# One pass of cluster products for the two-token pairs of the first batch, and a new order for the first quarter of the program

## The chip, the cores and the metric

The kernel runs on one core of one Trainium2 chip. A core has five engines, each with a queue of its own that it works through in order: TensorE (PE: matrix products, whose weight loads are shown apart as PEld), VectorE (DVE), ScalarE (ACT), GpSimd (POOL) and SyncE (SP, which issues most transfers). They wait for each other through semaphores. The metric is the device time of the one launch in microseconds (us), the median of the runs taken; lower is better.

## The reference

Two layers follow each other. The first is attention restricted by clusters, for 4 batches, 8 heads, 768 tokens and head size 64: every query and every key goes to the nearest of 16 centroids of its head (by cosine), and a query only sees keys of its own cluster.

```python
q_assign = np.argmax(np.einsum('bhsd,hcd->bhsc', q_n, c_n), axis=-1)
k_assign = np.argmax(np.einsum('bhsd,hcd->bhsc', k_n, c_n), axis=-1)
mask = q_assign[:, :, :, None] == k_assign[:, :, None, :]
scores = np.where(mask, scale * np.matmul(q, k.transpose(0, 1, 3, 2)), -1000000000.0)
attn = softmax(scores)            # written out with max, exp and sum
x = np.matmul(attn, v)            # then heads side by side: 3072 tokens x 512
```

The second layer takes each of the 3072 tokens through `h = x @ w_in` (512 to 1024), `u = h * softmax(h)`, a normalisation of u over its 1024 columns with gain `g_ln`, and `@ w_out` (1024 to 512).

## The kernel before, in words

**Tiles.** Work on q and k goes by pair: two heads of one batch, so 4 batches x 4 pairs. For each pair the kernel needs q and k with the head dimension on the partitions, as bf16, in a tile `qk` of its own (six of them in turn). Under the 64 rows of the head stand up to 32 further rows: the one-hot code of the token's cluster. A product over these 80 or 96 rows is then the score plus a constant (256) where query and key share a cluster, and the exponential's bias takes the constant away again; keys of other clusters vanish. That is the mask.

**From loaded q and k to scores.** The first batch (4 pairs) differs from the other three. Its pair 0 is prepared in two halves, from 64x64 transposes on PE (line 396). Pairs 1, 2 and 3 of the first batch are the ones that the change speaks of: each partition holds 12 tokens' data in one long row, which PE turns in 128x128 blocks (line 403, "tp" in the order), two tokens to a block, so the turned tile `xt` holds even tokens in its upper 64 rows and odd tokens in its lower 64, and the two heads lie side by side in its columns. The code calls them `twelve`; "two-token pairs" is meant by that. In the other batches DVE turns the data by itself (line 444), and the two heads lie one above the other.

For a pair the steps are, with the name each has in the order: copy out of PSUM into `xt` (xa, xb; lines 422 and 430; ACT or DVE), cast into `qk` (ca; lines 468 to 472; ACT, DVE or POOL), products with the centroids into the PSUM tile `csc` (cl; PE), a turn of `csc` in 32x32 blocks (tb; line 497; DVE), the maximum over each group of 16 (mx; line 510; DVE), the one-hot code (oh; line 515; DVE), a turn back (ot; line 521; DVE), four copies of the code into `qk` (pl; lines 533 to 540; POOL, DVE or a transfer), and a memset that blanks the 16 rows that belong to the other head (bl; line 549). Scores are S (line 627, PE), their exponential E (line 635, ACT), the product with v is V (line 654, PE), the division by the sum N (lines 666 and 679, DVE). In the second layer, h and y are PE's products, hm, u, bn and ag are DVE's, ex is ACT's, at and al are POOL's, sc is the scaling of the output.

In the products with the centroids (lines 475 to 492) four products stand beside each other in four 32-column strips of PE's array. For a two-token pair that takes two rounds, one for each head (`hh`), that add up in PSUM: 8 products of 384 columns. Lines 912 to 916 make the weights for it, 128 columns for each pair.

**Order.** Nothing is scheduled at run time. Every step is an entry with an engine, needs and a planned cost; the strings `ORDER` (line 28 on) say for each engine in which order kinds of steps stand in its queue, and `AWAY` moves single steps to another engine. `ca0.0.0.1.0` reads: cast, batch 0, pair 0, q, head 1, half 0. The costs and keys in the `add` calls only tell the recording layer in which sequence to write the program; an engine's own queue is set by `ORDER` and `AWAY` alone.

**Start.** Until the first q and k have landed, PE runs products of zeros (`idle`, line 859) into a PSUM tile that nobody reads: the step wm (25 of them, each 128 columns, with a weight load of 128 columns before each) and single steps fl of two each.

Of the kernel before, what the change touches and what calls it, by code (L numbers as in the profile page):

```python
# [22 lines left out]
class Weave:  # L23
# [6 lines left out]
        ld4 si ld3 lv lg ld3 lo lv lo ld2 lo2 lv ld6 lv ld8 li4 tx ld3 lv ld tx lv tu ld10 tx tu ld4  # L30
        tu lv ld ou lv ld3 tu ld3 ou ld8 ou2 ld2 tu ld5 tx lv2 ld pl tu ld10 tx ld5 ou2 tu lv tx lv
        tu ld9 ou tu ld4 lv2 ld4 pl tu ou tx ld3 tu tx ld4 ou tu2 ou lv tx lv ou pl3 tu3 ou tx2 ou2
        tu tx tu tx tu ou2 tx ou tu2 ou tu ou6
    """
    ORDER["POOL"] = """
        pl2 bl pl3 ca pl ca cv ca3 pl3 bl ca pl ca pl cv z2 pl3 ca bl z cv2 ca pl4 sg bl cv2 wi ca
        wi7 ca3 at pl4 z cv ca2 cv bl cv al pl2 ca3 at pl2 z bl ca3 al at al pl4 at ca cv ca cv ca
        cv al bl ca3 pl4 ca2 pl4 at2 pl2 bl ca cv pl al2 ca2 cv2 ca2 at cv ca4 al pl4 at2 cv bl cv3
        pl2 al pl2 ca2 bl ca at al ca pl2 cv2 pl ca3 al ca3 pl at2 pl3 al2 ca2 pl ca at cv pl cv at
        ca at cv al pl2 bl pl al at3 al2 at al2 at al at al2 at2 po at al3  # L40
    """
    ORDER["PE"] = """
# [126 lines left out]
def kernel(  # L169
# [80 lines left out]
    def used(hh):  # L250

        return slice(0, D + NC_) if hh == 0 else slice(0, D + 2 * NC_)
# [603 lines left out]
    def idle(n):  # L856

        for _ in range(n):
            nc.tensor.matmul(idle_p[:, :P], idle_w, idle_w)  # L859
# [465 lines left out]
```

## Time and profile before

| | |
|---|---|
| time, three runs | 223.49, 223.98, 224.14 us; median 223.98 |
| profiled execution: span from first to last instruction | 222.4 us |
| PE, DVE, ACT, POOL busy | 97%, 90%, 88%, 57% of the span |
| TensorE clock granted over the span | 0.999 |
| chain that ended last | PE 91%, DVE 3%, ACT 2%, issue 2% |

The profiled execution carries no time of its own beside its span; the median of the runs is 1.6 us above that span, which is what lies before the first and behind the last instruction together with the difference between executions. A row of a timeline gives start, length, engine, line, operation, output and inputs with sizes, and how many such instructions were merged; "x16" for 8 products is right, since each product of fp32 data leaves two records. Busy time counts an instruction from its start to its end, and ends of neighbours overlap, so the busy shares lie a little above the share of time in which an engine could have taken nothing more.

### The profile page before, as it was taken

The page shows a single profiled execution, that of the slowest core. Times are in us where ns is not written, and L with a number is a line of the kernel's source. Part 1 is how long each engine was busy: PE and PEld are TensorE (multiplying, and loading weights), DVE is VectorE, ACT ScalarE, POOL GpSimd, SP SyncE. Part 2 cuts the span into 40 slices and gives each one's busy share as a digit, 9 for nine tenths or more (in the row PEclk, how much of TensorE's full clock was granted, in tenths as well). Part 3 has the DMA queues.
Part 4 walks back from the last instruction along what each step waited for, and adds up shares of the span by engine and source line. Part 5 has one row for each costly group of instructions (what it writes and reads, how often), then busy time and mean ns, then how long its engine had stood idle before and what let it go on. Part 6 is the DMA issues. An engine that isn't in the chain of part 4 may idle for free.

```text
span 222.4 us, 6852 instructions
## 1 busy us (share of the span) xinstructions
PE 214.8 (97%) x2518; PEld 151.8 (68%) x2548; DVE 199.1 (90%) x363; ACT 194.7 (88%) x382; POOL 126.6 (57%) x252
## 2 busy tenths in 40 slices
PE   8999899999999999999999999999999999999993
PEld 7765577767777687777777666676767767665452
DVE  2789999999999999899989999999999979999891
ACT  3899999999999999999999989999999989795352
POOL 3189597759884986188837674783746101226131
PEclk9999999999999999999999999999999999999999
DMA  6998989797799979899999897998922928565623
GB/s 157 352 388 221 193 165 284 203 172 165 127 175 237 180 141 215 136 193 166 153 211 239 156 185 150 151 168 158 230 99 50 115 78 145 117 165 121 166 98 143
DMA packets 122433, 38.74 MB, mean 174 GB/s; under 512 B 111448, under 2 KB 117152, under 8 KB 122400
## 3 DMA queue, kind: packets, MB, share of 16 engines
q1 hardware_dynamic: 121680, 37.82, 79.8%
q10 hardware_dynamic: 720, 0.49, 0.7%
q8 instruction: 20, 0.33, 0.7%
q14 instruction: 13, 0.11, 0.1%
HBM read 23.11 MB, written 6.29 MB: 132 GB/s over the span
## 4 chain that ended last, share of the span: by engine, by line
PE 91%; DVE 3%; issue 2%; ACT 2%; DVEq 0%; ACTq 0%
PE sps L627 27%; PE hreg L744 18%; PE yps L813 17%; PE ops L654 16%; PE csc L489 4%; PE hreg L627 2%; PE idle_p L859 2%; PE csc L484 1%; PE hreg L403 1%; PE hreg L396 1%; ACT qk L468 1%; PE hreg L813 1%; ACT e L635 1%; DVE u L763 1%; DVE w_sum L598 1%
## 5 line engine op out<-in xcount | busy, mean ns | idle before, releaser
L635 ACT ACTIVATE e<-sps 128x512 bf16<-128x512 f32 (+1 forms) x276 | 143.2, 609 | 10.2 <-PE sps L627 9.8
L627 PE MATMUL sps<-qk 96*128 96x256 bf16 (+5 forms) x600 | 87.4, 263 | 0.7 <-ACT e L635 0.4
L627 PEld LDWEIGHTS <-qk 96*128 96x128 bf16 (+1 forms) x636 | 59.6, 121 | 24.5 <-issue 8.8
L654 PEld LDWEIGHTS <-e 128*128 128x128 bf16 x1152 | 49.9, 97 | 9.3 <-issue 1.9
L654 PE MATMUL ops<-v,e 128*128 128x65 bf16 x1152 | 54.3, 193 | 0.4 <-DVE x L679 0.4
L744 PE MATMUL hreg<-w_in_sb,xT 128*128 128x512 bf16 x177 | 48.3, 378 | 0.8
L813 PE MATMUL yps<-w_out_c,uT 128*128 128x512 bf16 x169 | 45.1, 379 | 0.8
L540 POOL COPY qk<-oht 32x384 f32<-32x384 f32 (+1 forms) x49 | 24.2, 494 | 21.5 <-DVE oht L521 15.7
L763 DVE TENSOR_TENSOR u<-e_sb,hreg 128x1024 bf16<-128x1024 bf16 (+1 forms) x25 | 29.1, 1169 | 2.7 <-ACT e_sb L756 2.1
L774 DVE BATCH_NORM_STATS2 bs<-u 128x6 f32<-128x512 bf16 x48 | 31.3, 677 | 0.0
L750 DVE TENSOR_REDUCE nmax<-hreg 128x1 f32<-128x1024 f32 x24 | 29.1, 1213 | 2.0 <-PE hreg L744 1.7
L756 ACT ACTIVATE e_sb<-hreg,nmax 128x1024 bf16<-128x1024 f32 x24 | 26.9, 1121 | 4.5 <-DVE nmax L750 4.4
L790 POOL TENSOR_SCALAR esq<-es,mv 128x1 f32<-128x1 f32 x24 | 8.3, 344 | 33.6 <-DVE mv L778 30.3
L813 PEld LDWEIGHTS <-uT 128*128 128x128 bf16 x200 | 18.0, 97 | 13.1 <-issue 0.3
L744 PEld LDWEIGHTS <-xT 128*128 128x128 bf16 x192 | 17.6, 97 | 11.3 <-ACT e L635 0.3
L472 POOL TENSOR_SCALAR qk<-xt 64x768 bf16<-64x768 f32 (+1 forms) x27 | 22.2, 823 | 3.5 <-DVE xt L444 1.7
L444 DVE STREAM_TRANSPOSE xt<-raw 128x768 f32<-128x768 f32 x24 | 22.2, 949 | 0.0
L470 POOL CAST qk<-xt 64x768 bf16<-64x768 f32 (+1 forms) x25 | 20.9, 836 | 1.2
L679 DVE TENSOR_TENSOR x<-ops,den 128x256 bf16<-128x256 f32 (+1 forms) x39 | 18.9, 486 | 1.3
L784 POOL TENSOR_SCALAR es<-esum 128x1 f32<-128x1 f32 x24 | 5.6, 236 | 20.9 <-ACT e_sb L756 20.4
L793 POOL TENSOR_TENSOR alpha<-esq,halves 128x1 f32<-128x1 f32 x24 | 13.8, 574 | 2.0
L830 ACT ACTIVATE y<-yps,alpha 128x512 f32<-128x512 f32 x15 | 10.4, 695 | 4.3 <-PE yps L813 3.0
(85 smaller groups left out, 206.9 us busy)
## 6 DMA issues: line engine op xcount, KB each, us to landing
vf<-in_v_dram SPq DMA_DIRECT2D x16, 384.0 KB, 4.6
out_dram<-y SPq DMA_DIRECT2D x23, 256.0 KB, 2.5
raw<-in_q_dram SPq DMA_DIRECT2D x50, 96.0 KB, 3.8
raw<-in_k_dram SPq DMA_DIRECT2D x50, 96.0 KB, 3.0
w_g<-in_moe_w_out_dram SPq DMA_DIRECT2D x4, 512.0 KB, 8.3
w_st<-in_moe_w_in_dram SPq DMA_DIRECT2D x4, 512.0 KB, 6.2
raw<-in_q_dram SPq DMA_DIRECT2D x3, 384.0 KB, 6.0
raw<-in_k_dram SPq DMA_DIRECT2D x3, 384.0 KB, 7.8
```

The source lines that it names most:

```text
L444: nc.vector.transpose(xt[:], raws[b, p, i][:].rearrange("p j c -> p (j c)"))
L472: VEC[e].tensor_scalar(dst, src, scalar1=inv_C, scalar2=1.0, op0=Alu.mult, op1=Alu.mult)
L540: ins = VEC[e].tensor_copy(dst.bitcast(F32), src.bitcast(F32).unsqueeze(1) .to_broadcast([NB, 2, n // 2]))
L627: ins = nc.tensor.matmul(sps_[n, k][:, c0:c0 + w], side(b, h // 2, 1, h % 2, keys)[r], side(b, h // 2, 0, h % 2, slice(s0 * P, s0 * P + w) ...
L635: ins = nc.scalar.activation(es[n, k][:, :w], sps_[n, k][:, :w], Act.Exp, scale=exp_scale, bias=-exp_scale)
L654: nc.tensor.matmul(opss[g][:, s, :VW], es[n, k][:, c0:c0 + P], v1[slot(b, h // 2)][:, h % 2, kt, :VW], start=(kt == 0), stop=(kt == n_t - 1))
L744: uses(nc.tensor.matmul(hreg[:, at(f, f2)[1], :], xTs[f][:, dc, :], w_in_sb[:, dc, f2 * FF2:(f2 + 1) * FF2], start=(dc == 0), stop=(dc == ...
L750: uses(nc.vector.tensor_reduce(ff[f, "nmax"][:], pair_of(f), axis=AXY, op=Alu.max, negate=True), *both(f))
L756: uses(nc.scalar.activation(ff[f, "e"][:], pair_of(f), Act.Exp, bias=ff[f, "nmax"][:], accum_out=ff[f, "esum"][:]), *both(f))
L763: uses(nc.vector.tensor_tensor(ff[f, "u"][:, r], ff[f, "e"][:, r], pair_of(f)[:, r], op=Alu.mult), *both(f)[r])
L774: nc.vector.bn_stats(ff[f, "bs"][:, f2, :], ff[f, "u"][:, f2, :])
L813: ins = nc.tensor.matmul(dst, ff[f, "uT"][:, at(f, f2)[0] * (n_fc // 2) + c, :], w_out_c[:, fc, cols], start=(fc == fcs[0] and turn == 0 i ...
```

## The change

It has five parts.

1. **One round of cluster products.** For a two-token pair the four products now take, for each of q and k, the columns of one head (`part`) with weights that serve the two tokens at once: `c_two`, 32 columns, the upper 64 rows for the even token, the lower 64 for the odd one. 4 products of 384 columns instead of 8. The result holds in each 32-row strip the scores of one head, 16 rows for even and 16 for odd tokens.
2. **The code is spread and turned at twice the width.** Since even and odd tokens of one head now share a strip, the one-hot step writes its groups of 16 into every other group of a 768-column tile (`apart`, zeroed once by POOL), and DVE turns 768 columns instead of 384 (`turned_apart`). The four copies then take 16 rows of 384 fp32 words instead of 32 rows, and write one head each; a score product of these pairs uses 80 rows for both heads, and the blanking memset of these three pairs is gone.
3. **The weights' own step** (cf) multiplies 128x256 instead of 128x512 elements, and POOL's memsets for it change.
4. **A new order for the first quarter** on all five engines, with 22 steps on other engines than before. Behind it the strings are the same as before.
5. **Idle products.** wm is 49 products of 64 columns instead of 25 of 128, each still with its weight load of 128 columns; the first score now also stands behind all idle products. The single steps fl are 10 (20 products) as before, at other places.

The planned costs of several POOL steps are also other numbers; they only act on the sequence of recording.

```diff
-    def used(hh):
-        return slice(0, D + NC_) if hh == 0 else slice(0, D + 2 * NC_)
+    def used(b, h):
+        return slice(0, D + NC_ * (1 if h % 2 == 0 or twelve(b, h // 2) else 2))
...
-    def clusters(b, p, hf, hh=None):
+    def clusters(b, p, hf):
         lo, n = (0, HALF) if hf is None else (hf * HALF, QTR)
-        if twelve(b, p):
-            for c in range(4):
-                i, part = divmod(c, 2)
-                nc.tensor.matmul(csc[c * NB:(c + 1) * NB, :], c_by_two[:, p, 2 * part + hh, :],
-                                 by_two(b, p, i)[:, hh].rearrange("p t n -> p (t n)"),
-                                 start=(hh == 0), stop=(hh == 1), tile_position=(0, c * NB))
...
+        for c in range(4):
             i, part = divmod(c, 2)
+            if twelve(b, p):
+                w = c_two[:, p, part, :]
+                x = by_two(b, p, i)[:, part].rearrange("p t n -> p (t n)")
+            else:
+                w, x = c_bd[:, p, :], xts[b, p, i][:, lo + part * n:lo + (part + 1) * n]
+            nc.tensor.matmul(csc[c * NB:(c + 1) * NB, :n], w, x, tile_position=(0, c * NB))
...
     def assign_hot(b, p, hf):
+        if twelve(b, p):
+            dst = apart.rearrange("p (u a c) -> p a u c", u=2, c=NB)[:, :, :, :NC_]
+            src, top = (x.rearrange("p (a u) c -> p a u c", u=2)
+                        for x in (by_group(b, p, hf, "cst"), spread_max(b, p, hf)))
...
     def assign_turn(b, p, hf):
+        if twelve(b, p):
+            asg[b, p, hf, "oht"] = turned_apart[:, p % 2, :]
+            nc.vector.transpose(turned_apart[:, p % 2, :], apart)
+            return
...
     def place(b, p, hf, i, part, e):
         if twelve(b, p):
-            ins = VEC[e].tensor_copy(
-                every_other(b, p, i, part)[D:D + NB].bitcast(F32),
-                src.bitcast(F32).rearrange("p (t n) -> p t n", t=n_t // 2).unsqueeze(1)
-                .to_broadcast([NB, 2, n_t // 2, P // 2]))
+            dst = (side(b, p, i, part, slice(0, S))[D:D + NC_].bitcast(F32)
+                   .rearrange("p (t u n) -> p u t n", u=2, n=P // 2))
+            src = asg[b, p, hf, "oht"][r.start:r.start + NC_, :].bitcast(F32)
+            ins = VEC[e].tensor_copy(dst, src.rearrange("p (u t n) -> p u t n", u=2, n=P // 2))
...
-    add("wm", "PE", 3.55, -1000, lambda e: idle(25))
+    add("wm", "PE", 3.55, -1000, lambda e: idle(49, 64))
...
-        aft = ["S{}.{}".format(*BANKS[i - 1])] if i else []
+        aft = ["S{}.{}".format(*BANKS[i - 1])] if i else [nm for nm in wv.by if re.match("wm|fl", nm)]
```

**Where the order moves.** First, PE from the second half of pair 0 on. In these rows the tile `raw` is the loaded q or k of pair 1 or later (turned three blocks at a time), `sps` the scores of pair 0. Before:

```order
L489 MATMUL csc<-xt,c_bd 32x192 x4
L859 LDWEIGHTS w_out_c
L859 MATMUL idle_p<-w_out_c 128x128
L859 LDWEIGHTS w_out_c
L859 MATMUL idle_p<-w_out_c 128x128
L403 MATMUL hreg<-ident_f,raw 128x128 x3
L627 LDWEIGHTS qk_99
L627 MATMUL sps<-qk_99 128x384
```

and now:

```order
L487 MATMUL csc<-xt,c_bd 32x192 x4
L404 MATMUL hreg<-ident_f,raw 128x128 x9
L868 LDWEIGHTS w_out_c
L868 MATMUL idle_p<-w_out_c 128x128
L868 LDWEIGHTS w_out_c
L868 MATMUL idle_p<-w_out_c 128x128
L635 LDWEIGHTS qk_99
L635 MATMUL sps<-qk_99 128x384
```

Nine turned blocks instead of three stand between the second cluster step of pair 0 and its first score (three more stand ahead of that cluster step), so all of pair 1 is turned before the first score. The cluster step of pair 1 then follows the fourth score, as 4 products; before, it followed the ninth, as 8.

Second, DVE behind the last one-hot code of pair 0. Here `csc` to `oht` are the steps of a cluster assignment, `qk_100` and `qk_101` are pairs 1 and 2. Before:

```order
L521 STREAM_TRANSPOSE oht<-oh 128x192
L430 COPY xt<-hreg 128x384 x3
L913 TENSOR_TENSOR w_out_c<-cps,w_out_c 128x512
L470 CAST qk_100<-xt 64x6x128
L549 MEMSET qk_99 16x192
L558 CAST v_0_105<-vf 128x6x64
L497 STREAM_TRANSPOSE cst<-csc 128x384
L510 TENSOR_REDUCE mx<-cst 128x24
L515 TENSOR_TENSOR oh<-cst,mx 128x384
L521 STREAM_TRANSPOSE oht<-oh 128x384
L470 CAST qk_100<-xt 64x6x128
L472 TENSOR_SCALAR qk_101<-xt 64x6x128
```

and now:

```order
L528 STREAM_TRANSPOSE oht<-oh 128x192
L431 COPY xt<-hreg 128x384
L557 MEMSET qk_99 16x192
L493 STREAM_TRANSPOSE cst<-csc 128x384
L548 COPY qk_99<-oht 32x2x96
L431 COPY xt<-hreg 128x384
L506 TENSOR_REDUCE mx<-cst 128x24
L596 COPY g_ln_115<-gps 128x8
L431 COPY xt<-hreg 128x384
L519 TENSOR_TENSOR w_out_c<-cst,mx 128x12x2x16
L525 STREAM_TRANSPOSE w_out_c<-w_out_c 128x768
L566 CAST v_1_106<-vf 128x6x64
```

The three casts of q and k leave DVE, and the weights' step is earlier and half as wide; the turn of pair 1's code is twice as wide.

Third, ACT from its third copy out of PSUM to the exponentials of pair 0. Before:

```order
L422 COPY xt<-ops 128x3x64
L468 ACTIVATE qk_99<-xt 64x384 x4
L635 ACTIVATE e<-sps 128x384 x6
L430 COPY xt<-hreg 128x384
L635 ACTIVATE e<-sps 128x384 x2
L430 COPY xt<-hreg 128x384
L635 ACTIVATE e<-sps 128x384
L430 COPY xt<-hreg 128x384
L468 ACTIVATE qk_101<-xt 64x6x128
```

and now:

```order
L423 COPY xt<-ops 128x3x64
L423 COPY xt<-hreg 128x3x64
L431 COPY xt<-hreg 128x384
L469 ACTIVATE qk_99<-xt 64x384
L431 COPY xt<-hreg 128x384 x3
L643 ACTIVATE e<-sps 128x384 x9
L431 COPY xt<-hreg 128x384
L643 ACTIVATE e<-sps 128x384 x3
```

Three of pair 0's half-wide casts leave ACT, and the four copies of pair 1 stand ahead of the first exponential.

More of the change, by code (lines that the diff above doesn't have):

```diff
@@ L1005 @@
                     cols = slice(0, S) if hf is None else slice(hf * HALF, (hf + 1) * HALF)
-                    costs = ({"POOL": 0.88, "ACT": 0.76, "DVE": 0.52 + 0.1 * i} if hf is None else
-                             {"POOL": 0.48, "ACT": 0.42, "DVE": 0.33})
+                    costs = ({"POOL": 0.79, "ACT": 0.76, "DVE": 0.52 + 0.1 * i} if hf is None else
+                             {"POOL": 0.45, "ACT": 0.42, "DVE": 0.33})
                     e = "ACT" if hf is not None and i == 1 else "POOL"
@@ L1018 @@
         for hh in range(2):
-            add(f"cv{t}.{hh}", "POOL", 0.455, first - 5,
+            add(f"cv{t}.{hh}", "POOL", 0.45, first - 5,
                 (lambda e, b=b, p=p, hh=hh: cast_v(b, p, hh, e)),
@@ L1032 @@
             old = last[-3] if len(last) >= 3 else None
[L1033 to L1039 removed]
+            add(f"cl{t}", "PE", 0.72 - 0.22 * hf if half else 0.87, first - 9,
+                (lambda e, b=b, p=p, hf=hf: clusters(b, p, hf)),
+                kept + ["cf" if twelve(b, p) else "cb"], take="m")
             add(f"tb{t}", "DVE", 0.37 if half else 0.56, first - 20,
@@ L1049 @@
                 nd += [nm for nm in wv.by if nm.startswith(f"pl{old}.")]
-            add(f"ot{t}", "DVE", 0.33 if half else 0.505, first - 9,
+            add(f"ot{t}", "DVE", 0.33 if half else 0.9 if twelve(b, p) else 0.505, first - 9,
                 (lambda e, b=b, p=p, hf=hf: assign_turn(b, p, hf)), nd)
@@ L1062 @@
                     lag=(1.0, 0.7))
-            add(f"bl{t}", "POOL", 0.27, first - 8 + 1.5,
-                (lambda e, b=b, p=p, hf=hf: blank(b, p, hf, e)),
-                [f"pl{t}.1.{part}" for part in range(2)], also={"DVE": 0.2})
+            if not twelve(b, p):
+                add(f"bl{t}", "POOL", 0.37, first - 8 + 1.5,
+                    (lambda e, b=b, p=p, hf=hf: blank(b, p, hf, e)),
+                    [f"pl{t}.1.{part}" for part in range(2)], also={"DVE": 0.2})
     ring_s, ring_e = 3, 9
@@ L1084 @@
                 ts = (f"{b}.{p}",) * 2
-            nd |= {f"pl{ts[1 - x]}.{x}.{part}" for x in range(2) for part in range(2)}
-            nd |= {f"bl{ts[0]}"} if hh else set()
+            nd |= {f"pl{ts[1 - x]}.{x}.{part}" for x in range(2)
+                   for part in ((hh,) if twelve(b, p) else range(2))}
+            nd |= {f"bl{ts[0]}"} if hh and not twelve(b, p) else set()
         nd = sorted(nd)
-        aft = ["S{}.{}".format(*BANKS[i - 1])] if i else []
+        aft = ["S{}.{}".format(*BANKS[i - 1])] if i else [nm for nm in wv.by if re.match("wm|fl", nm)]
         if (n, k) in slots:
@@ L1292 @@
     for z in range(1, R):
-        add(f"z{z}", "POOL", 0.25, 12 * z - 16, (lambda e, z=z: clear(z)))
+        add(f"z{z}", "POOL", 0.12, 12 * z - 16, (lambda e, z=z: clear(z)))
     wv.run()
```

156 lines of the change are left out of this document (73 added, 83 removed).

## The prediction

> **What bounds the kernel now.** I read the page first, then the busy time by stretches, then the chain of waits in order of time, then single groups and the timeline.
>
> ```profile
> span 222.4 us, 6852 instructions
> PE 214.8 (97%) x2518; PEld 151.8 (68%) x2548; DVE 199.1 (90%) x363; ACT 194.7 (88%) x382; POOL 126.6 (57%) x252
> PE 91%; DVE 3%; issue 2%; ACT 2%; DVEq 0%; ACTq 0%
> ```
>
> PE bounds the whole, so work taken off PE should count. The change lies in the first quarter, though, and up to DVE's last moved row (a turn of a code that ends at 57 us) the picture is another:
>
> ```profile
> core 0: us, PE busy (x) PEld busy (x) DVE busy (x) ACT busy (x) POOL busy (x), PEclk, DMA share, GB/s
> 10.00:20.00 10.00, 9.87 (x107) 7.11 (x107) 8.81 (x19) 9.96 (x26) 8.16 (x15) 1.00 0.96 327
> 20.00:30.00 10.00, 9.22 (x127) 5.80 (x127) 9.68 (x20) 9.52 (x21) 7.24 (x12) 1.00 0.93 213
> 10.00:57.00 47.00, 45.31 (x583) 32.64 (x586) 44.03 (x85) 46.08 (x100) 35.72 (x64) 1.00 0.92 226
> ```
>
> From 10 to 57 us PE, DVE and ACT are busy 45.31, 44.03 and 46.08 of 47 us: three engines at 96, 94 and 98%. From 20 to 30 DVE is fuller (9.68) than PE (9.22). The chain says the same:
>
> ```profile
> 13.68 1.43 PE csc L484 x16
> ...
> 19.68 0.82 DVE w_sum L595
> ...
> 20.52 1.19 DVE w_sum L598
> ...
> 23.40 0.56 DVE xt L430
> ...
> 24.09 0.60 PE hreg L627 x4
> ...
> 26.36 1.43 PE csc L484 x16
> ...
> 34.45 0.78 PE csc L489 x8
> ```
>
> Of the three double cluster steps two (13.68 and 26.36) stand on the chain. The third, at 20 us, is not there: from 19.68 to 24 us the chain runs on DVE, and PE's time there was free.
>
> **The change part by part.** *One round instead of two.* 8 products leave 16 records and hold the chain for 1.43 us; the later pairs' 4 products of the same 384 columns (34.45) hold it for 0.78. Each of the three steps gets 1.43 - 0.78 = 0.65 shorter: -1.95 us of PE work, -1.30 of it on the chain as it is now.
>
> *The start.* The first score moves:
>
> ```profile
> 8.66 0.72 PE L489 MATMUL csc<-xt,c_bd 128*32 128x192 f32 x7
> 9.90 0.48 PE L627 MATMUL sps<-qk 80*128 80x384 bf16 x2
> 12.69 0.66 PE hreg L403 x6
> ```
>
> Six turned blocks take 0.66 of the chain, 0.11 each. Behind the second cluster step (its end is 9.38, the next product can start at 9.31) stand nine blocks now, 0.99, and two idle products, some 0.1: the first score at 10.4 instead of 9.90, +0.5. But PE has then turned nine blocks more than before, which it need not do later, so the move is worth 0.5 - 0.99 = -0.5 to PE and is a loss of 0.5 only to what starts with the scores, ACT's exponentials. ACT gets work off in return:
>
> ```profile
> L468 ACT ACTIVATE qk<-xt 64x384 bf16<-64x384 f32 x6 | 3.0, 521 | 0.0
> 9.23 0.94 ACT qk L468 x2
> ```
>
> Three of these six casts go to POOL and DVE, 0.47 each by the chain: -1.4; one cast of 64x768 leaves and another comes. POOL, 35.72 of 47, covers what it receives; it loses three memsets and copies narrower strips. Were that cover gone, a cast late on POOL would hold the scores of its pair by its own length, some 0.5.
>
> *DVE.* Here the change adds. The rows:
>
> ```profile
> L444 DVE STREAM_TRANSPOSE xt<-raw 128x768 f32<-128x768 f32 x24 | 22.2, 949 | 0.0
> L521 DVE STREAM_TRANSPOSE oht<-oh 128x384 bf16<-128x384 bf16 x15 | 8.5, 565 | 0.1
> L497 DVE STREAM_TRANSPOSE cst<-csc 128x384 f32<-128x384 f32 x15 | 8.5, 567 | 0.9 <-PE csc L484 0.7 <-PE csc L489 0.2
> L470 DVE CAST qk<-xt 64x768 bf16<-64x768 f32 x4 | 2.3, 586 | 0.1
> L472 DVE TENSOR_SCALAR qk<-xt 64x768 bf16<-64x768 f32 x3 | 1.9, 631 | 0.0
> L913 DVE TENSOR_TENSOR w_out_c<-cps,w_out_c 128x512 f32<-128x512 f32 x1 | 0.7, 675 | 0.0
> L919 DVE TENSOR_TENSOR c_bd<-cps,own 128x128 f32<-128x128 f32 x1 | 0.3, 292 | 0.0
> L540 DVE COPY qk<-oht 32x192 f32<-32x192 f32 x2 | 0.5, 270 | 0.1
> L515 DVE TENSOR_TENSOR oh<-cst,mx 128x384 bf16<-128x384 f32 x15 | 8.4, 563 | 0.1
> L540 POOL COPY qk<-oht 32x384 f32<-32x384 f32 x43 | 22.2, 515 | 14.7 <-DVE oht L521 9.2 <-DVE den L666 3.4
> L533 POOL COPY qk<-oht 32x384 f32<-32x384 f32 x12 | 7.9, 662 | 2.9 <-DMA raw<-in_q_dram 2.3
> ```
>
> Gone are two casts (2 x 0.586), one scaled cast (0.631), the 512-wide product (0.675) and three turns (3 x 0.565): 4.17 us. New are three turns of 768 columns: bf16 and fp32 cost the same at 384 (0.565, 0.567), so I take the 0.949 of fp32 at 768, 2.85 together. The 256-wide product lies between 0.292 and 0.675, a third of the way: 0.42. One more memset and one more copy of 192 words, at most 0.27 each, 0.54. Two copies of 16x384 words have no row: at least the 0.27 of 192 words, at most POOL's 0.515 for 384; I take 0.47, the 192 words more at the slope that the narrow one bounds, 0.94 for both. The cast of 64x384 falls before 10 us, into DVE's wait for the first cluster step. Sum 4.75, so DVE gets +0.58 us. Not in it: the one-hot step writes every other group of 16. Lower bound nothing (the same 384 elements, 0.563); upper bound the ratio of POOL's copy to every other 64 words to its plain one, 662/515 = 1.29, 0.16 for each of three: +0.5. I take nothing, since DVE still reads and compares as many elements.
>
> *Idle products.* Their end sets when the first transposes start:
>
> ```profile
> 0.97 2.80 PEld L859 LDWEIGHTS <-w_out_c 128*128 128x128 bf16 x27 [0.97 <-DVE halves L863]
> 0.97 3.06 PE L859 MATMUL idle_p<-w_out_c 128*128 128x128 bf16 x27 [0.97 <-DVE halves L863]
> 5.72 1.06 PE L859 MATMUL idle_p<-w_out_c 128*128 128x128 bf16 x8
> 8.10 0.62 PE L859 MATMUL idle_p<-w_out_c 128*128 128x128 bf16 x8
> 24.97 0.73 PE L654 MATMUL ops<-v,e 128*128 128x65 bf16 x18
> L654 PE MATMUL ops<-v,e 128*128 128x65 bf16 x1152 | 54.3, 193 | 0.4 <-DVE x L679 0.4
> ```
>
> 27 products of 128 columns take 3.06 with the last one's length of about 0.3 in it: 0.106 each, 25 take 2.66. If half the columns take half the time, 49 take 2.61: -0.05. If weight loads set the pace, it is bounded by the value products, 65 columns with a full weight load each: (0.73 - 0.19)/17 = 0.032 at full clock. The first products run at half of that clock (8 idle products took 1.06 early, 0.62 later), so at most 0.064 x 49 = 3.1, +0.45. I take -0.05: a product of 64 columns at half clock, 0.053, is nearer to these rows' 0.106 halved than to the bound.
>
> The Trainium skill ("TensorE: Matmul & The Clock Gate", section "LDWEIGHTS (loading the stationary operand)") gives a weight load as its columns over 1.2 GHz, an estimate of 107 ns for 128 columns; 49 of them would be 5.2 us, and the sum 2.6 us worse. The value products' 0.032 speak against it here, and so does the same page's section on weight-path modes, where full-width bf16 loads are faster.
>
> *Loads.* On SP the last k of the first batch (pair 3) moves behind a v load and a w_out load.
>
> ```profile
> 7.10 0.65 SPq L377 DMA_DIRECT2D raw<-in_k_dram  x1
> 10.31 0.37 SPq L591 DMA_DIRECT2D w_g<-in_moe_w_out_dram  x1
> raw<-in_k_dram SPq DMA_DIRECT2D x3, 384.0 KB, 7.8
> 18.41 0.82 PE L403 MATMUL hreg<-ident_f,raw 128*128 128x128 f32 x6
> ```
>
> Issued at 7.10 and 7.8 us on its way, it is there at 15; at the place of the second w_out load, 10.31, it would be there at 18.1. PE turns it from 18.7 on (the last three of the six blocks at 18.41, then three more). Its cover is half a microsecond or so; each microsecond beyond holds PE as long, with only scores of pair 0 to do. The v loads and the other batches' q and k loads that move ahead of it gain slack. I take nothing for it and keep up to +0.5 for the range.
>
> *The sum.* PE alone would let the stretch shrink by 1.95, with the start by up to 2.4. DVE must then do 44.03 + 0.58 = 44.61 us in 47 - 1.95 = 45.05 us, 99%, which no stretch shows. At its fullest ten microseconds' share, 9.68 of 10, it needs 44.61/0.968 = 46.1 us: -0.9 us. Behind 57 us the orders are the same and PE sets the pace, so the lead stays. The profiled span would be 221.5, and against the runs, 223.98 - 0.9 = **223.1 us**.
>
> **The rivals.** *PE alone decides (chance 0.15):* the stall on DVE around 19 to 24 us came of the old order, where sums of w_out stood ahead of a division and a copy that PE needed; the new order puts them later. Then -1.95: 222.0. For it: the sums need w_out alone and can wait. Against it: of DVE's 2.97 idle us up to 57 it would use up 1.95 + 0.58.
>
> *The gain sits where nobody waits (0.20):* -1.30 on the chain, of which ACT's first exponential gives back 0.5 and DVE's added 0.58 more: -0.2, 223.8. For it: ACT is busy 46.08 of 47, the fullest of the three. Against it: ACT also loses 1.4 of casts.
>
> *DVE takes over (0.15):* it keeps its share of 44.03/47 = 93.7% because it still waits for PE in turn, and the spread one-hot write costs its upper bound. (44.61 + 0.5)/0.937 = 48.1, +1.1: 225.1, slower. The place is DVE between the two turns of 768 columns and the divisions behind them in its queue, for which value products wait; PE's gain is lost to it once DVE's added work exceeds what its idle 2.97 us leave beside PE's 1.95, about +1.0. For it: DVE's part of the chain from 19.68 us on; against it: +0.58 is little more than half of that.
>
> *Weight loads pace the idle products (0.05):* 2.80/27 = 0.104 for each load as issued above gives 49 x 0.104 = 5.1, 2.4 more than now, all of it ahead of the first transposes: 225.4. Against it are the value products.
>
> **How the numbers follow.** My forecast has 0.45, its own range being -0.4 to -1.4, 222.6 to 223.6. A measurement of this kernel tells 0.3%, 0.67 us, from no change. Faster by more: 0.36 of the forecast's 0.45, all of 0.15, 0.03 of the 0.20: 0.54. Within: 0.09 + 0.17 + 0.04 of DVE's case and 0.02 of the weight loads' = 0.32. Slower: 0.11 + 0.03 = 0.14. The range from 221.9 (PE alone) to 224.5 (halfway into DVE's case) leaves about 0.2 out.
>
> **What would show it.** In the changed profile: cluster steps of 8 records at about 0.78 in the chain; the first score near 10.4; turns of 768 columns near 0.95; copies of 16 rows at 0.27 to 0.515; idle products over by 4.0; DVE's busy share up to 57 us above 0.95 and fewer PE waits than now between 19 and 24 us. The forecast is wrong if the lead at the first product of the second layer's eighth token tile, far behind the moved part, is not the lead at the end, or if the spread one-hot write or the wide turn lies well above its row.

## The result, and the profile after

The changed kernel takes 225.29 us (median of five runs, 224.72 to 225.68) beside 223.91 us for the kernel before (five runs): ratio 1.0058, 95% interval 1.0041 to 1.0075. Run once more (six runs) it took 225.76 us, ratio 1.0085, 1.0063 to 1.0108. Forecast were 223.1 us and a range of 221.9 to 224.5. It got slower instead of faster, and the time lies outside the range; of the rivals, "DVE takes over" (225.1, chance 0.15) came nearest. Of some variants below a part of the executions ran at a lower granted clock (0.992 and less; 1 to 10 us longer, twice 86 and 91), so for these the text adds the median of the executions at 0.997 and more with their number, since the ratios of the new pass in the old order and of the hurried marks still hold some of the others.

From the page of the changed kernel:

```profile
span 222.9 us, 6842 instructions
PE 213.3 (96%) x2518; PEld 150.0 (67%) x2548; DVE 200.7 (90%) x365; ACT 194.1 (87%) x379; POOL 127.1 (57%) x246
PE 80%; DVE 7%; POOL 3%; issue 3%; DMA 3%; ACT 2%; SPq 0%; DVEq 0%; POOLq 0%; ACTq 0%
```

PE did get its relief (214.8 us before, 213.3 now). DVE has 1.6 us more than the 199.1 of before. PE's part of the chain of waits fell from 91% to 80% (84% in a second profile, see below), and DVE and POOL stand in it with 10% together. Busy time by stretches of the same kernel says where:

```profile
core 0: us, PE busy (x) PEld busy (x) DVE busy (x) ACT busy (x) POOL busy (x), PEclk, DMA share, GB/s
10.00:20.00 10.00, 9.86 (x101) 6.36 (x100) 8.63 (x21) 9.46 (x23) 7.72 (x15) 1.00 0.92 304
20.00:30.00 10.00, 8.65 (x115) 5.71 (x114) 9.58 (x20) 10.00 (x23) 7.90 (x13) 1.00 0.85 153
30.00:40.00 10.00, 8.43 (x126) 6.18 (x123) 9.73 (x17) 9.39 (x20) 8.17 (x13) 1.00 1.05 324
40.00:50.00 10.00, 9.79 (x147) 7.58 (x146) 9.90 (x20) 9.65 (x20) 9.03 (x16) 1.00 1.00 155
10.00:57.00 47.00, 43.61 (x556) 30.86 (x558) 44.61 (x86) 45.44 (x95) 34.16 (x56) 1.00 0.92 221
```

Of before, the prediction shows 10 to 30 us; the rows behind that are

```profile
30.00:40.00 10.00, 9.79 (x149) 7.47 (x147) 9.46 (x18) 10.00 (x22) 8.13 (x18) 1.00 0.96 247
40.00:50.00 10.00, 9.69 (x121) 6.79 (x119) 9.58 (x19) 9.60 (x21) 6.23 (x11) 1.00 0.90 163
```

From 20 to 40 us PE now has 2.9 us without work (1.0 before), and DVE is at 97% (96% before). Between 19 and 24 us PE's gap did close as forecast (busy 4.75 of 5 us, 4.31 before); it opens again behind that. PE waits for others there. Its waits between 10 and 57 us were these before,

```profile
PE hreg L627 <- DVE xt L430: 0.4, 1, 0.4
PE sps L627 <- ACT e L635: 0.4, 1, 0.4
PE ops L654 <- DVE x L679: 0.4, 1, 0.4
```

and now, with DVE's one long wait (us in all, times, longest):

```profile
PE sps L635 <- POOL qk L541: 1.8, 2, 1.1
PE ops L662 <- DVE x L687: 0.5, 2, 0.3
PE hreg L612 <- DVE w_sum L606: 0.4, 1, 0.4
...
DVE qk L557 <- POOL qk L548: 0.9, 1, 0.9
```

"Marks" are the one-hot codes that stand under q and k. The chain between 20 and 45 us runs over POOL's casts and copies of marks and then over DVE alone; its first row here is the cluster step of pair 1:

```profile
11.97 0.78 PE csc L487 x8
...
22.63 1.48 issue
24.12 0.94 POOL qk L541
25.11 1.17 POOL qk L471
26.32 0.83 POOL qk L471
...
29.67 0.97 DVE xt L445
30.64 0.95 DVE w_sum L606
31.59 0.89 DVE w_out_c L525
...
34.83 0.93 DVE w_sum L606
...
37.79 0.98 DVE w_sum L606
...
39.24 0.87 DVE oh L519
```

L525 at 31.59 is the turn of pair 3's code (into the spare part of w_out_c). It stands behind a division, a turn of fp32 data and a sum of w_out in DVE's queue. POOL's last two copies of these marks stand behind a memset and a cast of 64x768 (0.82 us) besides, and PE's longest wait (1.1 us, from 34.2) is for them.

How full DVE is shows best from its first turn of a two-token pair's products to the end of its last moved row. First before, then the change, then the change's second profile:

```profile
15.17:57.04 41.87, 40.31 (x542) 29.53 (x544) 39.82 (x75) 40.96 (x87) 32.17 (x56) 1.00 0.90 205
```

```profile
13.62:57.46 43.84, 40.54 (x530) 29.02 (x532) 42.62 (x79) 42.59 (x89) 30.93 (x50) 1.00 0.91 205
```

```profile
14.27:58.72 44.45, 40.82 (x533) 29.02 (x532) 43.23 (x79) 42.67 (x89) 31.76 (x50) 1.00 0.85 198
```

In these stretches DVE is idle for 2.05 us in 41.87 before, and for 1.22 in 43.84 and 44.45 after: it is busy 95.1% before and 97.2% after. The stretches don't hold the same steps (75 and 79 of DVE), so their work can't be subtracted; counted from the start of the span to the end of the last moved row, DVE has 48.68 us before, 50.02 and 50.63 after.

The exponentials of the scores show the course of the loss. Worked out from their starts in the traces, this is how much later (+) than in the kernel before the n-th one starts (us); the columns on the right belong to experiments below.

| n | change | change, second profile | new pass, old order | old pass, new order | change, half turns |
|---|---|---|---|---|---|
| 1 | +0.47 | +0.64 | -0.27 | +0.68 | +1.02 |
| 5 | +0.97 | +1.62 | -0.28 | +2.06 | +1.48 |
| 33 | -1.86 | -1.20 | -0.84 | +0.04 | -1.41 |
| 45 | -1.33 | -0.67 | -0.49 | +0.04 | -1.42 |
| 49 | -0.60 | +0.06 | +0.34 | +0.73 | -1.06 |
| 69 | -0.45 | +0.81 | +0.29 | +0.52 | -1.28 |
| 85 | +0.24 | +1.51 | +0.28 | +0.92 | -0.65 |
| last | +0.50 | +1.79 | +0.27 | +1.20 | -0.39 |

The change starts late, leads by up to 1.9 us at the 33rd, and loses the lead between the 33rd and the 85th, 29 to 57 us. Up to 44 us DVE is on the chain there. In both profiles 0.73 goes between the 45th and the 49th, where PE waits for pair 3's marks. Behind the 85th nothing moves much, as expected.

The two profiles of the same kernel differ by 1.3 us of span (222.9 and 224.2). Half of it comes at the start, as the first transposes show, first profile, then second:

```profile
3.91 0.62 PE L397 MATMUL hreg<-ident_f,raw 64*64 64x64 f32 x25
```

```profile
3.91 1.01 PE L397 MATMUL hreg<-ident_f,raw 64*64 64x64 f32 x25
```

25 transposes took 0.62 us in the one, 1.01 in the other, and 1.01 in the profile of before. In each trace's record of TensorE's granted clock, the full clock begins at 3.92 us in the first profile of the change, at 6.75 in the second and at 6.90 in before's. From the fifth to the 49th exponential the two profiles then lie 0.65 apart. The other 0.6 comes by the 69th: the product for the mean of w_out waits for the last sum of w_out, 0.4 us in the first profile, and in the second

```profile
PE hreg L612 <- DVE w_sum L606: 0.9, 1, 0.9
```

where the seven sums took 0.94 us each instead of 0.87. So the first profile, taken in the fastest of the five runs, flatters the change; beside before's profile belongs the second one, +1.8 us of span. For the three columns on the right of the table the full clock begins at 4.89, 5.37 and 3.95 us, so they too look up to some 0.7 us better at the start than at before's clock (an estimate from the 0.65 above).

### The profile page after: what moved, and what is told of

It is laid out like the page before. It is cut to its first block, busy times and chain, and to the rows that moved or that the text cites. A ratio compares the mean times of both kernels' runs of the same rounds, so it can differ in the third digit from the quotient of the medians.

```text
span 222.9 us, 6842 instructions
## 1 busy us (share of the span) xinstructions
PE 213.3 (96%) x2518; PEld 150.0 (67%) x2548; DVE 200.7 (90%) x365; ACT 194.1 (87%) x379; POOL 127.1 (57%) x246
## 4 chain that ended last, share of the span: by engine, by line
PE 80%; DVE 7%; POOL 3%; issue 3%; DMA 3%; ACT 2%; SPq 0%; DVEq 0%; POOLq 0%; ACTq 0%
PE sps L635 24%; PE hreg L752 18%; PE yps L821 17%; PE ops L662 14%; PE csc L487 4%; DMA raw<-in_q_dram 3%; DVE w_sum L606 2%; POOL qk L471 2%; POOL qk L541 1%; PE hreg L404 1%; DVE xt L445 1%; ACT xt L431 1%; PE hreg L821 1%; ACT e L643 1%; DVE w_out_c L615 1%
## 5 line engine op out<-in xcount | busy, mean ns | idle before, releaser
L643 ACT ACTIVATE e<-sps 128x512 bf16<-128x512 f32 (+1 forms) x276 | 142.7, 602 | 11.1 <-PE sps L635 10.4
L635 PE MATMUL sps<-qk 80*128 80x256 bf16 (+5 forms) x600 | 89.0, 263 | 2.2 <-POOL qk L541 1.8
L635 PEld LDWEIGHTS <-qk 80*128 80x128 bf16 (+1 forms) x636 | 59.6, 121 | 25.3 <-issue 10.6
L662 PE MATMUL ops<-v,e 128*128 128x65 bf16 x1152 | 55.0, 193 | 0.7 <-DVE x L687 0.5
L798 POOL TENSOR_SCALAR esq<-es,mv 128x1 f32<-128x1 f32 x24 | 8.2, 340 | 37.3 <-DVE mv L786 34.2
L471 POOL CAST qk<-xt 64x768 bf16<-64x768 f32 (+1 forms) x28 | 23.2, 828 | 4.6 <-ACT xt L423 3.2
L473 POOL TENSOR_SCALAR qk<-xt 64x768 bf16<-64x768 f32 (+1 forms) x29 | 23.4, 808 | 3.6 <-DVE xt L445 1.7
L838 ACT ACTIVATE y<-yps,alpha 128x512 f32<-128x512 f32 x15 | 10.4, 694 | 4.3 <-PE yps L821 3.0
```

What stands on the lines that cost most here:

```text
L471: VEC[e].tensor_copy(dst, src)
L635: ins = nc.tensor.matmul(sps_[n, k][:, c0:c0 + w], side(b, h // 2, 1, h % 2, keys)[r], side(b, h // 2, 0, h % 2, slice(s0 * P, s0 * P + w) ...
L643: ins = nc.scalar.activation(es[n, k][:, :w], sps_[n, k][:, :w], Act.Exp, scale=exp_scale, bias=-exp_scale)
L662: nc.tensor.matmul(opss[g][:, s, :VW], es[n, k][:, c0:c0 + P], v1[slot(b, h // 2)][:, h % 2, kt, :VW], start=(kt == 0), stop=(kt == n_t - 1))
```

## The experiments

Two theories stood at the start. **A:** DVE is full, and what the new form adds there eats PE's saving. **B:** the new order costs the time by its own waits (POOL's copies, the late start, a cast on ACT). Later expectations call A "D" and B "Q"; "P" there is that PE's saving never lay on the path. Ratios are to the kernel before, run beside each variant (223.7 to 224.1 us).

**New pass with the old order, old pass with the new order.** The tables ORDER and AWAY of one kernel were put into the other (here in words, the tables are left out):

```diff
-    ORDER, AWAY = tables of the change
-    add("wm", "PE", 3.55, -1000, lambda e: idle(49, 64))
+    ORDER, AWAY = tables of before, without the three memsets bl0.1 to bl0.3
+    add("wm", "PE", 3.55, -1000, lambda e: idle(25))
```

> The one-pass cluster products with the tables of before (order, engines, 25 idle products of 128 columns); only the three memsets that the new form no longer has are gone. Theory A, DVE is full and the new form costs it time: three turns 0.97 instead of 0.565 (+1.2), three one-hot writes 0.73 instead of 0.55 (+0.5), one product 0.42 instead of 0.68 (-0.25), together +1.5 us on an engine with 3 us of room that is all waiting in turn: slower than before by about 1, 224.9. Theory B, the new order is what costs (PE waits 1.8 us for POOL's copies of marks, DVE 0.95 us for POOL before 13.4 us, the first exponential 0.5 later): with the old order PE's saving of 1.95 shows, at least the 1.3 of it on the chain: 222.0 to 222.7.

> The two-round cluster products of before with the tables of the change (order, engines, number of idle pairs; the three memsets put behind the last copy of marks of each pair on POOL); the idle products ahead stay 25 of 128 columns. Theory A, DVE's added work costs: without it (1.5 us of DVE less than the changed kernel) the time falls back to about before, 223.8 to 224.3. Theory B, the order costs: its waits stay and PE has 1.95 more to do: 226.5 to 227.2.

Measured: 224.85 us, ratio 1.0055 (1.0025 to 1.0086), for the new pass in the old order, with a median of 224.46 (223.94 to 224.87) in eight of twelve; 225.34 us, 1.0079 (1.0053 to 1.0105), for the old pass in the new order. The first is 0.5 above before: a loss, as A said, but half of its size. The second is what neither said: the order alone, with DVE's total at 199.1 us as before, costs 1.4. The new pass on top of it costs 0.1 (with the same idle products, next run) to 0.4 more. So each part is a loss by itself, the order the larger one.

The trace of the old pass in the new order shows where a part of this goes:

```profile
PE sps L629 <- POOL qk L535: 1.2, 1, 1.2
```

This wait ends at 36.6 us with the last copies of pair 3's marks, behind the same memset and cast on POOL, and its exponentials lose 0.69 between the 45th and the 49th as the change's do. DVE is not full in this kernel: from 10 to 57 us it is busy 42.65 of 47 us. So the wait for these marks comes with the order, without the wide turns.

**The idle products, and the change once more.**

```diff
-    add("wm", "PE", 3.55, -1000, lambda e: idle(49, 64))
+    add("wm", "PE", 3.55, -1000, lambda e: idle(25))
```

> The changed kernel with 25 idle products of 128 columns ahead of the data instead of 49 of 64. In the changed kernel's profile the 49 and the first pair took about as long (3.01 us with the last one's length) as the 27 of before (3.06). Theory: this part is worth nothing, 225.0 to 225.6 like the changed kernel. Rival: the weight loads or the clock at the start make it a loss, then 224.7 or less.

> The changed kernel once more, for a second profile. The first one was the fastest of five executions (224.72 of 224.72 to 225.68) and its TensorE clock rose at about 4 us, before's at about 6.9. Theory: the clock's rise falls at another time in another execution, and an execution in which it comes later is longer by 0.5 to 1: median 225.3 again, the second profile with a span of 223.3 to 223.8. Rival: the start has no part in the spread, then a late rise goes with a span of 222.9 as well.

Measured: 225.44 us, 1.0077 (1.0054 to 1.0100), with 25 products of 128 columns; 225.76, 1.0085 (1.0063 to 1.0108), for the change again, its profile with a span of 224.2. The idle products are worth nothing within the spread of some 0.3 us, and the second profile has the late clock and the longer time that the expectation had, by 1.3 us of span instead of 0.5 to 1.

**Three waits of the new order, put back one at a time.** The cast of 64x768 from ACT back to POOL; pair 3's marks hurried on DVE and POOL; the first two scores and exponentials ahead.

```diff
 AWAY: "ACT"
-        ca0.0.0.0.0 ca0.2.1.0 ca1.1.0.1 ca3.2.0.1 ...
+        ca0.0.0.0.0 ca0.2.1.0 ca3.2.0.1 ...
```

> The changed kernel with one step put back: the cast of 64x768 of the second batch's pair 1 (k, even head, ca1.1.0.1) that the change had given to ACT goes back to POOL, behind its twin. In the second profile of the changed kernel the exponentials lose 0.96 us against before between the 77th and the 81st, where ACT does that cast; POOL is busy 2.1 of 7 us there. Theory Q (the new order's queues cost the time): 0.8 to 0.95 faster than the changed kernel, 224.6. Theory D (DVE is full and sets the end of the moved stretch): ACT's cast lies beside DVE's work, not over 0.3 gained, 225.2.

```diff
 ORDER["DVE"]
-        ... tb xt mx oh N xt su ot N pl ...
+        ... tb xt mx oh ot N xt su N pl ...
 ORDER["POOL"]
-        ... ca cv ca pl sg ca pl2 wi ...
+        ... ca cv ca pl3 sg ca wi ...
```

> The changed kernel with pair 3's marks hurried: on DVE their turn of 768 columns stands right behind their one-hot step (before: behind a division, a turn of 768 fp32 columns and a sum of w_out), on POOL the last two copies of marks stand ahead of a memset and a cast of 64x768. In the changed kernel PE waits 1.06 us for such a copy at 34.2 us and the exponentials lose 0.73 between the 45th and the 49th. Theory Q: the 0.7 comes back, 224.8. Theory D: what DVE does earlier here it does later there; the wait comes back at another of its steps, under 0.3 gained.

```diff
 ORDER["PE"]
-        ... fl4 cl tp3 fl S2 cq tp S2 cl S2 ...
+        ... fl4 cl tp fl S2 tp2 cq tp S2 cl S2 ...
 ORDER["ACT"]
-        ... xa2 ca xa3 E9 xa ...
+        ... xa2 ca xa E2 xa2 E7 xa ...
```

> The changed kernel with its first two scores put ahead of six of the nine turned blocks of pair 1 that stand before them, and the first two exponentials ahead of ACT's two copies of these blocks. The first exponential of the change starts 0.6 later than before's at the same clock, the fifth 1.6. If the late start is paid at the end: 0.5 faster, 224.9. If DVE sets the end of the stretch whatever the start: no difference from the change, 225.2 to 225.7.

Measured: 225.59 us, 1.0083 (1.0062 to 1.0105), for the cast and 225.47, 1.0075 (1.0055 to 1.0095), for the earlier scores: neither run gained. Without the cast the exponentials lost the same time a little later, waiting for PE. The earlier scores leave the late start itself untested: the first exponential starts 0.18 later than before's, but the fifth is still 1.57 late. The hurried marks gave a median of 227.54 us and 1.0057 (1.0027 to 1.0088), and in four of twelve 224.19 to 224.82, about 1.0 below the change. In these four B's 0.7 comes back and a little more; as a whole the variant is not faster than the change.

**DVE without the sums of w_out, before and changed.**

```diff
         else:
-            nc.vector.scalar_tensor_tensor(out=w_sum[:], in0=w_g[:, fc, :], ...)
+            pass
```

> The kernel before without seven of the eight steps that add up w_out (scalar_tensor_tensor of 128x512, 5.9 us of DVE between 20 and 37 us; the mean of w_out is then that of its first row block). What DVE's fullness costs the kernel before: PE waits 1.7 us from 10 to 57 us, so at most about 1.5 faster; I expect 222.8 to 223.4 by either theory.

> The changed kernel without the same seven steps (6 us and more of DVE less). Theory D: with DVE relieved PE's saving of 1.95 appears, so this stands 1.0 to 1.9 below the kernel before without the sums, 221.2 to 222.0, and 3 or more below the changed kernel. Theory Q: the waits behind POOL's copies, ACT's cast and the late start stay, so it stays above the kernel before without the sums by 0.5 or more and gains under 1 on the changed kernel, 224.5 to 225.

Both leave out seven of the eight additions for the mean of w_out. Measured: 223.26 us, 0.9970 (0.9956 to 0.9984), and 223.75 us, 1.0000 (0.9983 to 1.0018), with 223.68 in ten of twelve. Before gains 0.7 to 0.8 from 5.9 us less on DVE, the change 1.5 to 2.0. DVE weighs more on the change than on before, as A said; but the change stays 0.4 above the other kernel without sums, where A had it 1.0 to 1.9 below and B 0.5 or more above. The exponentials of the two say where: the change's fifth is 2.2 later than the other's, its 69th level with it, its 85th 0.85 later. So a saving does appear (2.2 made up), and the late start has spent it beforehand. The 0.85 behind the 69th falls where ACT's moved cast stands:

```profile
50.09 1.73 ACT L639 ACTIVATE e<-sps 128x512 bf16<-128x512 f32 x3
51.84 0.84 ACT L469 ACTIVATE qk<-xt 64x768 bf16<-64x768 f32 x1
52.59 2.50 ACT L639 ACTIVATE e<-sps 128x512 bf16<-128x512 f32 x5
```

ACT works through without a gap here. The same cast was worth nothing in the full change; that it costs once DVE is out of the way is read from this trace, and no run took the cast out here.

**The old order, tuned for the new pass.** First only pair 3's turn behind its one-hot step, then also a cast from DVE to POOL's idle time with sums moved later; and that cast alone in the kernel before.

```diff
 ORDER["DVE"]
-        ... cv ot su N su2 tb mx N oh su ot N xt2 N ...
+        ... cv ot su N su2 tb mx N oh ot N su xt2 N ...
```

> The one-pass products with the order of before (as in the first of these runs), and one more swap on DVE: the turn of pair 3's marks right behind their one-hot step and ahead of a division and a sum of w_out (0.98 us there). That kernel led before by 0.85 us up to its 41st exponential and lost 1.2 up to the 49th, where PE waited 1.36 us for POOL's first copy of these marks, 0.5 us after the turn. If this wait alone takes the lead away: 0.8 less than that kernel, 223.6 to 224.0. If DVE is full and only hands the wait on: 224.4 to 224.9.

```diff
 AWAY: "DVE"
-        ... ca0.1.0.0 ca0.1.0.1 ca0.2.1.1 ...
+        ... ca0.1.0.0 ca0.1.0.1 ...
```

> The same, and DVE relieved: the cast of pair 2's k (odd head, 0.86 us there) goes to POOL, which is idle for 2.7 us around 23 us, and the second sum of w_out goes behind the division that stood behind it, with two later sums moved likewise. If DVE's fullness keeps the saving of the one-pass products hidden, 0.86 us less on DVE gives 0.5 to 0.9 more than the run without it: 222.8 to 223.3, faster than before. If PE and ACT are the bound by then: as the run without it.

> The kernel before with only that cast moved from DVE to POOL (no one-pass products). 5.9 us of DVE less, the sums, gave it 0.8; 0.86 less gives at most that, likely 0.1 to 0.4: 223.6 to 223.9. It tells whether a gain of the run beside it comes from the one-pass products or from the cast.

Measured: 224.61 us, 1.0023 (1.0007 to 1.0038), with 224.27 in nine of twelve, 0.2 below the run without the swap and between its two forecasts; 224.72, 1.0034 (1.0019 to 1.0049); and 223.74, 0.9996 (0.9985 to 1.0008). In the old order DVE mostly hands the wait on: PE waited 1.36 us for POOL's copy without the swap, and with it

```profile
PE ops L661 <- DVE x L686: 1.5, 3, 0.6
```

1.5 us for divisions on DVE. The cast to POOL, and the sums moved later, gave nothing (0.4 more than the run before it): up to the 45th exponential that kernel leads by 2.05, by the 49th by 0.93 and by the 69th by 0.21, with PE's mean of w_out waiting 0.7 us for the last sum.

**The new form's work on DVE, taken out and put in.** Only half of each spread code is turned, so the marks of half of the groups stay zero; or the kernel before turns 256 columns more behind each of its three turns.

```diff
-            nc.vector.transpose(turned_apart[:, p % 2, :], apart)
+            nc.vector.transpose(turned_apart[:, p % 2, :HALF], apart[:, :HALF])
```

> The one-pass products with the order of before, but the three turns of pair 1 to 3's codes turn only the first 384 of the 768 spread columns (the marks of half of the groups are then zero; a memset on POOL ahead of the data clears the turned tile). 3 x (0.97 - 0.565) = 1.2 us of DVE less. Theory D, DVE's work between 14 and 57 us sets when the stretch ends: 0.8 to 1.2 below the same kernel with whole turns, 223.2 to 223.6 and faster than before. Theory P, the saving on PE never lay on the path, whatever DVE does: within 0.3 of that kernel, 224.3 to 224.9.

> The kernel before, with one turn of 256 bf16 columns more behind each of the three turns of pair 1 to 3's codes, into a tile nobody reads: some 0.4 each, 1.2 to 1.3 us of DVE in all, about what the wide turns add. Theory D: before's DVE has 2.0 us of idle time from 15.2 to 57.0, of which PE's waits leave little: 0.5 to 1.2 slower, 224.4 to 225.1. Theory P: no difference, 223.7 to 224.1.

> The changed kernel with the same half turns (marks of half of the groups zero). Its DVE idles 1.22 us between 14.3 and 58.7, less than in any other of these kernels. Theory D: 0.8 to 1.2 less, 224.2 to 224.7. Theory P, or a theory in which the late start or ACT sets the end: within 0.3 of the change, 225.2 to 225.7.

Measured: 223.73 us, 0.9990 (0.9976 to 1.0003), with 223.69 in eleven of twelve, for half turns in the old order; 224.25, 1.0009 (0.9996 to 1.0021), with 224.14 in eleven of twelve, for the added turns; 224.10, 1.0008 (0.9995 to 1.0021), for half turns in the change. The added turns took 0.402 us each, 1.2 together. The half turns bring the change back to before, 1.2 to 1.7 down, a little over what A gave; in the old order they bring 0.8. Put into the kernel before, the same amount costs 0.2 to 0.3, which the interval does not tell from nothing, and less than A gave. That before had about 1 us of room on DVE is one reading. The other is that the added turns stand behind the turn of the marks and delay no marks, while the half turns bring each pair's marks 0.4 us earlier; no run tells the two apart. Together with the four kernels above (medians as said above):

| | old pass | new pass, half turns | new pass |
|---|---|---|---|
| old order | 223.9 | 223.7 | 224.5 |
| new order | 225.3 | 224.1 | 225.3 to 225.8 |

The order's cost is not one number: 1.4 with the old pass, 0.8 to 1.3 with the new one, 0.4 with half turns.

**Are the order's cost and the turns' cost one?**

The hurried marks once more, and hurried marks and half turns together:

> The changed kernel with pair 3's marks hurried, once more, since only four of its twelve executions ran at the full clock (224.19 to 224.82). If these four tell the truth, the place of pair 3's marks on DVE and POOL is 1.0 of what the change costs: 224.2 to 224.8 again, and in the profile no loss of 0.7 between the 45th and the 49th exponential. If DVE only hands the wait on: 225.2 to 225.8.

> The changed kernel with both named causes taken away: pair 3's marks hurried, and the half turns (marks of half of the groups zero, 1.2 us of DVE less). If the two are separate costs of 1.0 and 1.3, this ends at 223.0 to 223.4, below before, and what is left of PE's 1.95 is seen. If both are the same cost (DVE's time ahead of the turn of pair 3's marks), it ends where the half turns alone ended, 223.9 to 224.3.

Measured: the hurried marks again 226.29 us, 1.0085 (1.0059 to 1.0112), with four of twelve from 224.20 to 225.76; over both runs of this kernel eight of 24 count, with a median of 224.4. With half turns as well 224.32 us, 1.0021 (1.0000 to 1.0042), with 224.0 in ten of twelve. So hurried marks alone take about 1.0 off the change, half turns alone 1.2 to 1.7, and both end where half turns alone ended (0.3 and 0.1 above before). The two are not separate costs. PE's wait for pair 3's marks fits that: 1.1 us in the change, 0.8 with half turns, none with both. Read with the 1.2 us of the old pass in the new order, pair 3's marks come too late, by what the new order puts ahead of them on DVE and POOL, and by the wider turns. That this wait is the larger part of the loss rests on eight executions of 24; the half turns also take work off all of DVE's queue.

No version that does all the work was faster than the kernel before; the 223.74 of before with one cast moved is no difference.

## Why the prediction was wrong

*One round instead of two: right.* The cluster step stands in the chain with 0.78 and eight records, as forecast, and with half turns the new pass is worth 225.3 to 224.1 in the new order.

*The idle products: right.* The 49 and the first pair took 3.01 us as forecast (over by 3.98), and putting the old ones back changed nothing. *The loads: right;* in neither profile of the change was pair 3's k waited for.

*The start: right in place, too small.* The first score came at 10.47 in the first profile, 10.4 forecast, but that profile had the earlier full clock; in the second, with nearly before's clock, it came at 10.82. The loss for ACT was 0.97 and 1.62 by the fifth exponential, not 0.5. What the late start costs the full change stays open: it is made up by the 33rd exponential, but with the sums taken out of both kernels its 2.2 us were missing.

*DVE: the term that was too small.* Forecast +0.58 us. Over the whole program DVE's busy time rose by 1.6 in the first profile, and by 2.3 in the second (whose figure for PE has 30 products more on record than the other two pages and can't be set beside them):

```profile
PE 215.8 (96%) x2548; PEld 150.6 (67%) x2548; DVE 201.4 (90%) x365; ACT 194.4 (87%) x379; POOL 128.1 (57%) x246
```

0.36 of it is the cast of 64x384, which was put ahead of 10 us and left out of the sum, and 0.3 lies behind the last moved row. The rest, 1.0 and 1.6, stands in groups of the changed kernel up to 57 us:

```profile
L606 DVE SCALAR_TENSOR_TENSOR w_sum<-w_g,g_ln,w_sum 128x512 f32<-128x512 f32 x7 | 6.1, 869 | 0.1
...
L541 POOL COPY qk<-w_out_c 16x384 f32<-16x384 f32 x10 | 6.2, 621 | 3.5 <-DVE w_out_c L525 3.1
...
L525 DVE STREAM_TRANSPOSE w_out_c<-w_out_c 128x768 bf16<-128x768 bf16 x3 | 2.9, 970 | 0.0
...
L519 DVE TENSOR_TENSOR w_out_c<-cst,mx 128x384 bf16<-128x384 f32 x3 | 2.2, 729 | 0.0
...
L519 DVE TENSOR_TENSOR oh<-cst,mx 128x384 bf16<-128x384 f32 x2 | 1.4, 706 | 0.0
...
L541 DVE COPY qk<-w_out_c 16x384 f32<-16x384 f32 x2 | 1.2, 590 | 0.1
```

The turns were priced right (0.949 taken, 0.970). The spread one-hot step took 0.73 instead of 0.55, +0.53 for three; the prediction held +0.5 as its upper bound and took nothing. That the bound fits is luck: it came from POOL's strided copies, and the plain one-hot steps of 384 elements got longer just as much (0.55 before, 0.71 now), which had no price at all. The sums went from 5.9 to 6.1 us, 6.6 in the second profile. The two copies of 16 rows took 0.59 instead of the 0.47 taken, +0.24, and POOL's ten 0.62, above the 0.515 bound: narrower strips save POOL little against the 0.66 of before. The three casts that left were dearer than priced (2.06 us, 1.80 taken), which gives back 0.26.

*The step from DVE's work to the time failed.* The sum let DVE work at its fullest ten microseconds' share, 44.61/0.968 = 46.1. DVE did reach 97%, but only from 13.6 us on; over the sum's own stretch, from 10 us to the last moved row, it was busy 45.07 of 47.46 us and, in the second profile, 46.29 of 48.72: 95.0% both times. At that share even the forecast work needs 47.0 us, no gain, and with 1.0 to 1.6 for 0.58 it is 47.4 to 48.0, +0.4 to +1.0.

*The order: the term that stood at nothing.* The sum priced the moved rows by their durations and looked at waits only at the start and for the loads. The new order cost 0.8 to 1.3 us with the new pass, and 1.4 with the old one and no more work on DVE. The sum did not ask what stands ahead of pair 3's turn on DVE, and between its copies on POOL, in the new order: PE waits 1.1 to 1.2 us there. The lower share of DVE and these waits are two views of one thing in part, so the two terms can't be added.

*The rival "DVE takes over"* had the right place, DVE between the wide turns and the divisions, and a chance of 0.15. That its 225.1 lies so near is partly luck: its share of 93.7% is lower than the 95.0%, its bound for the one-hot step came from another engine's copies, and it had no term for the order.

*The rival "the gain sits where nobody waits"* may have a part too, which no run shows by itself: in the old order with half turns 0.2 is all that is left of 1.95, within the noise. In that kernel ACT is busy 46.55 of 47 us:

```profile
10.00:57.00 47.00, 44.91 (x565) 32.12 (x564) 45.20 (x86) 46.55 (x101) 35.65 (x62) 1.00 0.93 229
```

What stays open: the rest of the 1.4 that the new order costs with the old pass, beside the 0.7 that its exponentials lose at pair 3's marks; what the late start costs; whether the half turns help by DVE's time or by earlier marks; and how much of the 0.7 us by which DVE's total differs between two executions of the change comes from what POOL happens to do beside it.

## What to carry to other kernels

Where three engines are busy 94 to 98% of a stretch, work taken off one of them is worth what the other two leave, and work added to another counts the more, the less room it has and the more others wait behind it (here 1.2 us of turns counted 0.2 to 0.3, 0.8, and 1.2 to 1.7); price the added work first. A moved step costs by what it is put in front of, even where the total work stays the same: list what stands ahead of the step that others wait for, on each queue that it crosses. And a price read from a row holds only with the neighbour that the row had.

## What the runs showed of the hardware

The spread write of the one-hot step costs nothing by itself. In the kernel before, the plain one took 0.55 us with POOL idle from 22.95 to 25.23:

```profile
23.86 0.55 DVE L515 TENSOR_TENSOR oh<-cst,mx 128x384 bf16<-128x384 f32 x1
```

With the new pass in the old order, the spread instruction took three durations. DVE's and POOL's rows of that kernel's timeline, in pairs; first with POOL idle from 22.42 to 25.11:

```profile
23.33 0.55 DVE L518 TENSOR_TENSOR w_out_c<-cst,mx 128x384 bf16<-128x384 f32 x1
```

```profile
21.60 0.82 POOL L470 CAST qk<-xt 64x768 bf16<-64x768 f32 x1
25.11 0.93 POOL L540 COPY qk<-w_out_c 16x384 f32<-16x384 f32 x1 [2.69 <-DMA raw<-in_q_dram]
```

Then beside POOL's casts, plain or scaled:

```profile
15.46 0.92 DVE L518 TENSOR_TENSOR w_out_c<-cst,mx 128x384 bf16<-128x384 f32 x1
...
29.61 1.20 DVE L518 TENSOR_TENSOR w_out_c<-cst,mx 128x384 bf16<-128x384 f32 x1
```

```profile
14.24 1.73 POOL L472 TENSOR_SCALAR qk<-xt 64x768 bf16<-64x768 f32 x2
15.92 1.14 POOL L470 CAST qk<-xt 64x768 bf16<-64x768 f32 x1
...
29.07 0.82 POOL L472 TENSOR_SCALAR qk<-xt 64x768 bf16<-64x768 f32 x1
...
29.90 1.27 POOL L565 CAST v<-vf 128x384 bf16<-128x384 f32 x2
```

0.55 alone, 0.92 and 1.20 beside casts, of which one took 1.14 instead of 0.82 itself. The division x<-ops,den of 128x256, with one input in PSUM, took 0.42 in each of its nine cases between 10 and 57 us, POOL busy or not. This is what the Trainium skill says ("SBUF — State Buffer", section "Who interferes with whom"): a DVE instruction with two inputs in SBUF and a POOL instruction that reads SBUF hold each other off for the whole instruction. The traces agree as far as they go: the step is stretched by 0.37 and 0.65 us where a cast of POOL was under way when it began, and not where POOL is idle; in the kernel before, a plain one that began 0.1 us ahead of a cast of 64x768 took 0.56, and the cast 1.14. The prediction did not weigh this. Whether this contention makes a part of the change's loss was not tested: no run took it away by itself.
